# Order of stores and loads on one queue, y's parts in two portions, a fifth product read through a copy, and a denser first pair

## The chip, the cores and the metric

The kernel runs on one core of one Trainium2 chip. TensorE (PE) multiplies matrices into PSUM banks, VectorE (DVE), ScalarE (ACT) and GpSimd (POOL) work on tiles, and SyncE (SP) issues most of the DMAs. The metric is the device time of one execution in microseconds; lower is better.

## The reference

Three stages follow one another on 3072 tokens of 512 features. The stage that the change is about is the last, here called MoE2.

```python
for t in range(S):                                   # per head, decayed linear attention
    state = gamma * state + k_t (outer) v_t
    y[t] = scale * q_t @ state
h = x @ w_in;  x = (h - tanh(h)) @ w_out             # MoE1, d_ff = 2048
h = x @ w_in2                                        # MoE2, d_ff = 1024
e = exp(h - max(h));  sm = e / (sum(e) + 1e-9)
solu = h * sm
ln = (solu - mean(solu)) / sqrt(var(solu) + 1e-6) * g_ln
out = ln @ w_out2
```

## The kernel before

All products are made as three matmuls of a high and a low part each (hi x hi, hi x lo, lo x hi). MoE2 works on 12 pairs of 128-token tiles; pair j has the odd tile 2j+1 and the even tile 2j.

*First product of MoE2.* `Pair.part` makes the 7 products P1, P2, P6, P5, P7, P4, P3 of a Strassen scheme; each is `product2` (L922), 6 matmuls of 128x512 into a PSUM bank. Bank q1 gathers P1, P6 and P7 on top of one another, bank q3 gathers P5 and P3. After P1, P6 and P7 `keep2` (L929) has ScalarE copy q1 as it then is to a tile `part`. `add_half` (L937) has VectorE add a bank and a `part` to one half of a tile hn of h, with its minimum (nm). After P7 VectorE makes the odd tile's second half from q3 (then P5 alone) and P7's copy, so P3, which goes on in q3, has to wait for that reading.

*The middle.* `soft` makes exp (ScalarE, L947), the product with h (VectorE, L949), hn (ScalarE, L951), the squares (ScalarE, L953) and a block transpose (VectorE, L955), stores the tile to memory as `ud` (SyncE, L956), and GpSimd ends with the row scale `sc`. `turn` (L969) loads it back as hn<-ud in the transposed order, 128x32x32. `trans` splits it into uh (a ScalarE cast, L160) and ul (VectorE, L161).

*Second product.* `outp` is 24 matmuls into po (L986), three for each of 8 slices: uh, uh, ul. ScalarE scales the result to ob (L990) and issues the DMA to out.

*Inputs of a pair.* `load_y` (SyncE, L468) loads yl, `sum_y` has GpSimd make ysum from it (four instructions, L482 to L485), and `split_y` splits both: ScalarE casts yha (2 instructions) and yhs (one, 128x1024, L498), GpSimd subtracts for yla (3) and yls (4, L475). ya serves P1, P2 and P4, ys serves P5, P6, P7 and P3.

*Order.* Pair 0 lies between the last steps f of MoE1's second product (`products_y`, 12 matmuls a step, L377); ysb are ScalarE's and VectorE's copies of its PSUM banks. Pairs 1 to 11 come behind it: TensorE's order is that of the code (`manual_schedule`): pair j, then the two output tiles of pair j-1, up to pair 9; then pair 10, pair 11 and all the outputs left. On the other engines a scheduler sets the order; `pin` keeps an instruction where the code has it among others pinned on its engine.

Of the kernel before, what the change touches and what calls it, by code (L numbers as in the profile page):

```python
# [26 lines left out]
F32 = mybir.dt.float32  # L27
# [9 lines left out]
P = 128  # L37
# [51 lines left out]
def body(ctx: ExitStack, tc, z, w_in, w_out, w_in2, w_out2, g_ln, cst, tab, out):  # L89
# [14 lines left out]
    def t4(shape, dtype, name):  # L104
        return big.tile(shape, dtype, tag="t4", name=name)
# [365 lines left out]
    def on_pool(n, out, a, b, op):  # L471
        k = out.shape[1] // n
        for i in range(n):
            at = slice(i * k, (i + 1) * k)
            nc.gpsimd.tensor_tensor(out[:, at], a[:, at], b[:, at], op)  # L475

    def sum_y(j):
        t = yl[j]
        a11, a12, a21, a22 = (t[:, i, k : k + 2, :] for i in range(2) for k in (0, 2))
        s = ysum[j] = t4([P, 4, 2, P], F32, "ysum")  # L480
        s1, s2, s3, s4 = (s[:, i, :, :] for i in range(4))
        nc.gpsimd.tensor_tensor(s1, a21, a22, ALU.add)  # L482
        nc.gpsimd.tensor_tensor(s2, s1, a11, ALU.subtract)
        nc.gpsimd.tensor_tensor(s3, a11, a21, ALU.subtract)
        nc.gpsimd.tensor_tensor(s4, a12, s2, ALU.subtract)  # L485

    def split_y(j):
        t, s = yl.pop(j), ysum.pop(j)
        a22 = t[:, 1, 2:4, :]
        ya, ys_ = ([t4([P, 4, 2, P], F32R, f"y{n}{g}") for n in "hl"] for g in "as")  # L490
        flat = "p a k t -> p (a k t)"
        for to, lo, n, src in (
            (ya, 0, 2, t[:, 0, :, :].rearrange("p k t -> p (k t)")),
            (ya, 2, 1, a22.rearrange("p k t -> p (k t)")),
            (ys_, 0, 4, s.rearrange(flat)),
        ):
            h, o = (w[:, lo : lo + n, :, :].rearrange(flat) for w in to)
            nc.scalar.copy(h, src)  # L498
            on_pool(n, o, src, h.bitcast(F32), ALU.subtract)
        at = {P1: (ya, 0), P2: (ya, 1), P4: (ya, 2)}  # L500
        at |= {P5: (ys_, 0), P6: (ys_, 1), P7: (ys_, 2), P3: (ys_, 3)}
        ys[j] = {m: [w[:, i, :, :] for w in to] for m, (to, i) in at.items()}


    wl, xs, sums = {}, {}, {}
# [410 lines left out]
    def product2(j, m, ph, first=True):  # L916
        a = ys[j][m]
        n = 0
        for r in range(2):
            bh, bl = com.w[m, r]  # L920
            for x, w in ((a[0], bh), (a[0], bl), (a[1], bh)):
                nc.tensor.matmul(  # L922
                    ph, x[:, r, :], w, start=first and n == 0, stop=n == 5, skip_group_check=True
                )
                n += 1
# [9 lines left out]
    def add_half(h, half, ph, part, seen):  # L935
        hn, nm = h
        nc.vector.tensor_tensor_reduce(  # L937
            hn[:, half * 512 : (half + 1) * 512], ph, part, -1.0,
            3.0e38 if seen is None else nm[seen], ALU.add, ALU.min, nm[half],
        )  # L940

    def soft(i, h, last):

        hn, nmx = h[0], h[1][last]
        ex = t4([P, FF2], F32, "ex")
        ssum = sp.tile([P, 1], F32, tag="ssum", name="ssum")
        nc.scalar.activation(ex, hn, AF.Exp, bias=nmx, scale=-1.0, accum_out=ssum)  # L947
        us = sp.tile([P, 1], F32, tag="us", name="us")
        nc.vector.scalar_tensor_tensor(ex, hn, 1.0, ex, ALU.mult, ALU.mult, accum_out=us)  # L949
        nc.vector.tensor_scalar(us, us, -1.0 / FF2, None, ALU.mult)  # L950
        nc.scalar.activation(hn, ex, AF.Identity, bias=us)  # L951
        ssq = sp.tile([P, 1], F32, tag="ssq", name="ssq")
        nc.scalar.activation(ex, ex, AF.Square, bias=us, accum_out=ssq)  # L953

        nc.vector.transpose(ex, hn)  # L955
        nc.sync.dma_start(out=ud[i], in_=ex)  # L956

        nc.vector.tensor_scalar(ssum, ssum, 1e-9, -1.0, ALU.add, ALU.mult)
        nc.vector.reciprocal(ssum, ssum)
        nc.vector.tensor_scalar(ssq, ssq, ssum, ssum, ALU.mult, ALU.mult)  # L960
        nc.vector.tensor_scalar(ssq, ssq, 1.0 / FF2, 1e-6, ALU.mult, ALU.add)
        sc = sp.tile([P, 1], F32, tag="sc", name="sc")
        nc.gpsimd.tensor_tensor(sc, ssq, mhalf, ALU.pow)
        nc.gpsimd.tensor_tensor(sc, sc, ssum, ALU.mult)
        uc[i], sc2[i] = hn, sc

    def turn(j):
        for i in (2 * j + 1, 2 * j):
            nc.sync.dma_start(  # L969
                out=uc[i].rearrange("p (c i b) -> p c i b", c=NF2, i=B),  # L970
                in_=ud[i].rearrange("(i a) (g c b) -> (a g) c i b", i=B, g=4, c=NF2),
            )

    def trans(i):
        u = uc.pop(i)
        uh, ul = (t4([P, NF2 * P], F32R, "u" + n) for n in "hl")
        parts(uh, ul, u, nc.vector)
        ut[i] = [w.rearrange("p (f t) -> p f t", f=NF2) for w in (uh, ul)]
# [15 lines left out]
    class Pair:  # L994
# [5 lines left out]
        def part(self, m):  # L1000
            j = self.j
            if m == P1:
                self.q1 = bank2()
                product2(j, P1, self.q1)
                self.kept = keep2(self.q1)
            elif m == P2:
                q = bank2()
                product2(j, P2, q)
                add_half(self.b, 0, q, self.kept, None)
            elif m == P6:  # L1010
                product2(j, P6, self.q1, False)
                self.u2 = keep2(self.q1)
            elif m == P5:
                self.q3 = bank2()
                product2(j, P5, self.q3)
            elif m == P7:
                product2(j, P7, self.q1, False)
                self.kept = keep2(self.q1)
                add_half(self.a, 1, self.q3, self.kept, None)
            elif m == P4:  # L1020
                q = bank2()
                product2(j, P4, q)
                add_half(self.a, 0, q, self.kept, 1)
                soft(2 * j + 1, self.a, 0)
            else:
                product2(j, P3, self.q3, False)
                add_half(self.b, 1, self.q3, self.u2, 0)
                soft(2 * j, self.b, 1)
                ys.pop(j)
# [5 lines left out]
    for n, (s, f) in enumerate(steps):  # L1035
        if n:
            if f == 0:
                y_banks(s)
                if s == NSB - 1:
                    bank_of[:] = [(ps_a, "r"), (ps_a, "r"), (ps_h, "h"), (ps_h, "h")]  # L1040
            load_g(n + 5)
            load_wo(n + 4)
            if n + 2 < len(steps):
                split_p(n + 2)
            if n + 2 < NF1:
                split_wo(n + 2)
            products_y(f, gp.pop(n), wo[f], py)
        if f == NF1 - 1:
            keep_y(s, py)
        if s >= NSB - 3 and n % 2 == 0 and com.n[2] < 12:  # L1050
            com.step()
        m = n - 2 * NF1 - 6
        if m >= 0 and m % 3 == 0:
            step2(m // 3)
        if s == NSB - 1:
            if f == 0:
                load_y(0)
            if f == 2:
                sum_y(0)
                load_y(1)  # L1060
            if f == 5:
                split_y(0)
            if f == 9:
                sum_y(1)
                load_y(2)
            if f == 8:
                pair = Pair(0)
            for m in {8: (P1, P2), 9: (P6,), 10: (P5,), 11: (P7,), 12: (P4,), 13: (P3,)}.get(f, ()):
                pair.part(m)
            if f == 12:  # L1070
                split_y(1)
            if f == 13:
                turn(0)
            if f == 14:
                sum_y(2)
    G.close()
    M.close()


    ps_2 = ctx.enter_context(tc.tile_pool(name="ps_2", bufs=6, space=PSUM, reuse_waits="tile"))  # L1080
    ps_o = ctx.enter_context(tc.tile_pool(name="ps_o", bufs=2, space=PSUM, reuse_waits="tile"))
    NJ = NTT // 2
    bank_of[:] = [(ps_2, "h2")]
    load_y(3)
# [1 line left out]
    def pair_of(j, before):  # L1086
        pair = Pair(j)
        for n, m in enumerate((P1, P2, P6, P5, P7, P4, P3)):
            if n == 0 and j + 1 < NJ:
                split_y(j + 1)  # L1090
            if n == 2 and j + 2 < NJ:
                sum_y(j + 2)
            if n == 4 and j + 3 < NJ:
                load_y(j + 3)
            if n == 5 and before is not None:
                trans(2 * before + 1)
            pair.part(m)
        turn(j)
        if before is not None:
            trans(2 * before)  # L1100
# [75 lines left out]
```

## Time and profile before

| | us |
|---|---|
| median of 3 runs | 865.69 |
| the 3 runs | 864.72 to 869.44 |
| profiled execution | 867.15 |
| its span | 865.4 |
| TensorE busy in the span | 829.4 (96%) |
| VectorE, ScalarE, GpSimd busy | 540.7, 461.2, 291.6 |

The span is the time from the first to the last recorded instruction. An engine's row in a timeline gives its start, its duration and, in brackets, how long the engine had been idle before it and what ended that. A row with x2 stands for two instructions that follow one another.

### The profile page before, as it was taken

What the parts mean: (1) busy time and instruction counts of PE and PEld (TensorE: products, weight loads), DVE (VectorE), ACT (ScalarE), POOL (GpSimd) and SP (SyncE); (2) the same over time, 40 slices, a digit from 0 to 9 for tenths busy, and PEclk for the clock granted to TensorE, in tenths of its full rate; (3) what the DMA queues carried; (4) which work ended last, traced back from release to release, by engine and by line L of the source; (5) the groups of instructions that cost most, each with busy time, mean ns of one, the idle gap of its engine ahead of it and who ended that gap; (6) DMA issues with size and microseconds to landing.
All of it is one profiled execution on the core that took longest, in us unless ns stands there. A gap on an engine that the chain in (4) does not pass through costs nothing.

```text
span 865.4 us, 16366 instructions
## 1 busy us (share of the span) xinstructions
PE 829.4 (96%) x6296; PEld 675.4 (78%) x6296; DVE 540.7 (62%) x999; ACT 461.2 (53%) x868; POOL 291.6 (34%) x304
## 2 busy tenths in 40 slices
PE   5799999999999899999999999999899999999898
PEld 4678888788877687888788888888577777777786
DVE  3788975999858757223573979473555455555561
ACT  4655744646555546444462627244566666666662
POOL 4411100180634348433300350142544444444210
PEclk9899999999999899999999999999899999999999
DMA  9658654344899626955584647440766666665574
GB/s 361 254 215 301 254 190 156 120 147 177 303 362 335 236 82 223 411 198 174 195 337 127 226 121 281 148 169 25 171 145 147 147 147 145 146 147 122 121 162 105
DMA packets 168460, 169.41 MB, mean 196 GB/s; under 512 B 105664, under 2 KB 117952, under 8 KB 168384
## 3 DMA queue, kind: packets, MB, share of 16 engines
q1 hardware_dynamic: 160032, 153.38, 57.1%
q10 hardware_dynamic: 8352, 15.00, 4.7%
q8 instruction: 49, 0.80, 0.4%
q14 instruction: 27, 0.22, 0.1%
HBM read 107.02 MB, written 61.34 MB: 195 GB/s over the span
## 4 chain that ended last, share of the span: by engine, by line
PE 81%; DVE 5%; DMA 4%; ACT 3%; issue 3%; POOL 2%; SPq 0%; ACTq 0%; POOLq 0%; DVEq 0%
PE py L377 29%; PE ph L750 15%; PE po L986 14%; PE ph L922 11%; PE ph L352 8%; PE out L228 2%; DMA hn<-ud 2%; PE sc L228 2%; DMA z<-z 1%; DMA raw<-w_in 1%; ACT part L929 1%; POOL hs L768 1%; DVE hn L937 1%; POOL yls L475 1%; ACT uh L160 0%
## 5 line engine op out<-in xcount | busy, mean ns | idle before, releaser
L377 PE MATMUL py<-gp,w 128*128 128x512 f32 x768 | 175.4, 389 | 0.0
L377 PEld LDWEIGHTS py<-gp,w 128*128 128x128 f32 x768 | 144.1, 188 | 29.9
L986 PE MATMUL po<-w,uh 128*128 128x512 f32 x384 | 118.6, 390 | 0.0
L768 POOL TENSOR_TENSOR hs<-hs,th 128x512 f32<-128x512 f32 x48 | 66.8, 1395 | 95.8 <-ACT th L766 91.1
L986 PEld LDWEIGHTS po<-w,uh 128*128 128x128 f32 x384 | 72.1, 188 | 14.8
L352 PE MATMUL ph<-xh,w 128*128 128x512 f32 x256 | 82.1, 395 | 0.8 <-DVE w L154 0.8
L377 PE MATMUL py<-gh,w 128*128 128x512 f32 x256 | 79.2, 390 | 0.3 <-ACT gh L365 0.3
L986 PE MATMUL po<-w,ul 128*128 128x512 f32 x192 | 76.4, 398 | 0.6 <-DVE us L950 0.6
L153 ACT CAST w<-wf 128x512 fp32r<-128x512 f32 x70 | 43.1, 621 | 57.6 <-DVE wf L144 47.1
L922 PE MATMUL ph<-w,yhs 128*128 128x512 f32 x192 | 63.9, 416 | 6.4 <-ACT part L929 5.8
L475 POOL TENSOR_TENSOR yla<-yl,yha 128x256 fp32r<-128x256 f32 x36 | 26.3, 756 | 127.2 <-ACT yha L498 127.2
L766 ACT ACTIVATE th<-hs 128x512 f32<-128x512 f32 x48 | 30.3, 631 | 60.4 <-DVE hs L776 52.4
L937 DVE CUSTOM_DVE_ANT_0 hn<-ph,part 128x512 f32<-128x512 f32 x24 | 16.6, 691 | 72.5 <-ACT part L929 54.9
L154 DVE TENSOR_TENSOR w<-wf,w 128x512 fp32r<-128x512 f32 x70 | 51.2, 736 | 15.3 <-ACT w L153 14.5
L161 DVE TENSOR_TENSOR gp<-g,gp 128x512 fp32r<-128x512 f32 x64 | 48.4, 770 | 18.8 <-ACT gp L160 18.6
L750 PE MATMUL ph<-xh,wch 128*128 128x512 f32 x140 | 57.3, 409 | 1.6 <-DVE hs L776 1.6
L352 PEld LDWEIGHTS ph<-xh,w 128*128 128x128 f32 x256 | 48.0, 188 | 11.8 <-DVE w L154 1.3
L377 PEld LDWEIGHTS py<-gh,w 128*128 128x128 f32 x256 | 48.0, 188 | 10.6 <-ACT gh L365 0.7
L929 ACT COPY part<-ph 128x512 f32<-128x512 f32 x36 | 21.1, 586 | 64.7 <-PE ph L922 64.7
L750 PE MATMUL ph<-xh,wcl 128*128 128x512 f32 x140 | 55.4, 396 | 0.0
L750 PE MATMUL ph<-xl,wch 128*128 128x512 f32 x140 | 55.3, 395 | 0.0
L776 DVE TENSOR_TENSOR hs<-ph,part 128x512 f32<-128x512 f32 x48 | 32.9, 686 | 35.2 <-PE ph L750 20.8
(123 smaller groups left out, 1811.9 us busy)
## 6 DMA issues: line engine op xcount, KB each, us to landing
z<-z SPq DMA_DIRECT2D x48, 512.0 KB, 6.4
g<-gd SPq DMA_DIRECT2D x64, 256.0 KB, 5.3
raw<-w_in SPq DMA_DIRECT2D x24, 512.0 KB, 6.3
raw<-w_out SPq DMA_DIRECT2D x24, 512.0 KB, 4.4
gd<-hs SPq DMA_DIRECT2D x48, 256.0 KB, 3.9
ud<-ex SPq DMA_DIRECT2D x24, 512.0 KB, 4.5
hn<-ud SPq DMA_DIRECT2D x24, 512.0 KB, 5.8
y1d<-ysb SPq DMA_DIRECT2D x24, 256.0 KB, 3.9
```

The source lines that it names most:

```text
L153: pin(nc.scalar.copy(hi, wf), fixed)
L154: pin(eng.tensor_tensor(lo, wf, hi.bitcast(F32), ALU.subtract), fixed)
L161: eng.tensor_tensor(o, src, h.bitcast(F32), ALU.subtract)
L228: pin(nc.tensor.matmul(o, a, b, start=True, stop=True, skip_group_check=True), held[0])
L352: nc.tensor.matmul(ph, a[:, k, :], x, start=n == 0, stop=n == 3 * NK - 1), s < 2
L377: nc.tensor.matmul(py[e], a[:, cols], x, start=f == 0 and n == 0, stop=f == NF1 - 1 and n == 2)
L475: nc.gpsimd.tensor_tensor(out[:, at], a[:, at], b[:, at], op)
L750: nc.tensor.matmul(ph, a, x, start=first and n == 0, stop=n == 5, skip_group_check=True)
L768: eng.tensor_tensor(g, h, th, ALU.subtract)
L776: nc.vector.tensor_tensor(h, ph, part, ALU.add)
L922: nc.tensor.matmul(ph, x[:, r, :], w, start=first and n == 0, stop=n == 5, skip_group_check=True)
L986: nc.tensor.matmul(po, a[:, f, :], b, start=f == 0 and n == 0, stop=f == NF2 - 1 and n == 2)
```

## The change

Four things are changed. `pin` is put around the stores `ud` and the loads of hn, so that SyncE issues both stores of a pair, then both loads, then yl. `split_y` gets an argument for its two portions: portion 0 (yha, yla) is asked for after P1 of the pair before, portion 1 (yhs, yls) after P6, and `sum_y` after P7. P5's result is copied by ScalarE (`p5`), and the odd tile's second half is made from q1 and that copy. The first pair takes four steps of products_y (P1 P2, P6 P5, P7 P4, P3) where it took six, with its other calls moved to match, and the two PSUM pools of the last stage are opened in the other order.

```diff
-    def split_y(j):
-        t, s = yl.pop(j), ysum.pop(j)
...
+    def split_y(j, halves=(0, 1)):
         flat = "p a k t -> p (a k t)"
...
+        for g in halves:
+            y = [t4([P, 4, 2, P], F32R, f"y{n}{'as'[g]}") for n in "hl"]
+            if g:
+                todo = ((0, 4, ysum.pop(j).rearrange(flat)),)
+                at = {P5: 0, P6: 1, P7: 2, P3: 3}
+            else:
+                t = yl[j]
+                todo = (
+                    (0, 2, t[:, 0, :, :].rearrange("p k t -> p (k t)")),
+                    (2, 1, t[:, 1, 2:4, :].rearrange("p k t -> p (k t)")),
+                )
+                at = {P1: 0, P2: 1, P4: 2}
+            for lo, n, src in todo:
+                h, o = (w[:, lo : lo + n, :, :].rearrange(flat) for w in y)
+                nc.scalar.copy(h, src)
+                on_pool(n, o, src, h.bitcast(F32), ALU.subtract)
+            ys.setdefault(j, {}).update({m: [w[:, i, :, :] for w in y] for m, i in at.items()})
...
-        nc.sync.dma_start(out=ud[i], in_=ex)
+        pin(nc.sync.dma_start(out=ud[i], in_=ex))
...
-            nc.sync.dma_start(
+            pin(nc.sync.dma_start(
                 out=uc[i].rearrange("p (c i b) -> p c i b", c=NF2, i=B),
                 in_=ud[i].rearrange("(i a) (g c b) -> (a g) c i b", i=B, g=4, c=NF2),
-            )
+            ))
...
                 product2(j, P5, self.q3)
+                self.p5 = keep2(self.q3)
             elif m == P7:
                 product2(j, P7, self.q1, False)
                 self.kept = keep2(self.q1)
-                add_half(self.a, 1, self.q3, self.kept, None)
+                add_half(self.a, 1, self.q1, self.p5, None)
...
-            if f == 5:
+            if f == 4:
                 split_y(0)
+            if f == 6:
+                sum_y(1)
             if f == 9:
-                sum_y(1)
                 load_y(2)
...
-            for m in {8: (P1, P2), 9: (P6,), 10: (P5,), 11: (P7,), 12: (P4,), 13: (P3,)}.get(f, ()):
+            for m in {8: (P1, P2), 9: (P6, P5), 10: (P7, P4), 11: (P3,)}.get(f, ()):
                 pair.part(m)
+            if f == 9:
+                split_y(1)
+            if f == 11:
+                sum_y(2)
             if f == 12:
-                split_y(1)
-            if f == 13:
                 turn(0)
-            if f == 14:
-                sum_y(2)
...
+    ps_o = ctx.enter_context(tc.tile_pool(name="ps_o", bufs=2, space=PSUM, reuse_waits="tile"))
     ps_2 = ctx.enter_context(tc.tile_pool(name="ps_2", bufs=6, space=PSUM, reuse_waits="tile"))
-    ps_o = ctx.enter_context(tc.tile_pool(name="ps_o", bufs=2, space=PSUM, reuse_waits="tile"))
...
-            if n == 0 and j + 1 < NJ:
-                split_y(j + 1)
-            if n == 2 and j + 2 < NJ:
+            if n == 5 and before is not None:
+                trans(2 * before + 1)
+            pair.part(m)
+            if n in (0, 2) and j + 1 < NJ:
+                split_y(j + 1, (n // 2,))
+            if n == 4 and j + 2 < NJ:
                 sum_y(j + 2)
             if n == 4 and j + 3 < NJ:
                 load_y(j + 3)
-            if n == 5 and before is not None:
-                trans(2 * before + 1)
-            pair.part(m)
         turn(j)
```

The first place is ScalarE's order where products_y ends and pair 1 begins. ph_6969 is bank q1 of pair 1 in the kernel before, so its three copies are those of P1, P6 and P7; yhs is that of pair 2.

```order
L498 CAST yha<-yl 128x256
L387 COPY ysb<-py 128x512 x2
L951 ACTIVATE hn<-ex,us 128x1024
L953 ACTIVATE ex,ssq<-ex,us 128x1024
L498 CAST yhs<-ysum 128x1024
L929 COPY part<-ph_6969 128x512 x3
L160 CAST uh<-hn 128x1024
```

In the changed kernel ph_6957 is q1 and ph_6996 is q3.

```order
L954 ACTIVATE hn<-ex,us 128x1024
L956 ACTIVATE ex,ssq<-ex,us 128x1024
L387 COPY ysb<-py 128x512 x2
L932 COPY part<-ph_6957 128x512
L503 CAST yhs<-ysum 128x1024
L932 COPY part<-ph_6957 128x512
L932 COPY part<-ph_6996 128x512
L932 COPY part<-ph_6957 128x512
L160 CAST uh<-hn 128x1024
```

The copy of P1's result moves from behind the yhs cast to ahead of it, pair 0's last hn and Square move ahead of the ysb copies, and the copy of P5 is new.

The second place is SyncE's order in a steady pair (pair 5, tiles 11 and 10). ud11 and ud10 are the stored tiles, hn what is loaded from them.

```order
L956 DMA ud11_148<-ex_7769 128x1024
L969 DMA hn_7689<-ud11_148 128x32x32
L956 DMA ud10_147<-ex_7794 128x1024
L468 DMA yl_7931<-y1d4_135 128x1024
L969 DMA hn_7692<-ud10_147 128x32x32
```

In the changed kernel:

```order
L959 DMA ud11_148<-ex_7781 128x1024
L959 DMA ud10_147<-ex_7806 128x1024
L972 DMA hn_7699<-ud11_148 128x32x32
L972 DMA hn_7702<-ud10_147 128x32x32
L468 DMA yl_7954<-y1d4_135 128x1024
```

The second store moves ahead of the first load, and the second load ahead of yl.

At the same place of a steady pair (pair 2) VectorE makes the halves of hn. In the kernel before ph2_7184 is q3, part_7199 is P7's copy, and ph2_7206 holds P4; the bracket names the engines that a row waits for.

```order
L937 ISA hn_7134,nm_7136<-ph2_7184,part_7199 128x512 [waits Activation_49]
L937 ISA nm_7136 128x1
L937 ISA hn_7134,nm_7135<-ph2_7206,part_7199,nm_7136 128x512 [waits DVE_49,PE_49]
L937 ISA nm_7135 128x1
L161 TENSOR_TENSOR ul_7203<-hn_6949,uh_7202 128x1024 [waits DMAHW3_49,Activation_49]
```

In the changed kernel ph2_7144 is q1, part_7190 the copy of P5 and part_7198 that of P7.

```order
L940 ISA hn_7138,nm_7140<-ph2_7144,part_7190 128x512 [waits Activation_49]
L940 ISA nm_7140 128x1
L940 ISA hn_7138,nm_7139<-ph2_7212,part_7198,nm_7140 128x512 [waits DVE_49,PE_49]
L940 ISA nm_7139 128x1
L161 TENSOR_TENSOR ul_7209<-hn_6951,uh_7208 128x1024 [waits DMAHW4_49,Activation_49]
```

The first half reads q1 in place of q3; its place and the engine that it waits for stay.

The third place is ScalarE's order from the end of pair 10 to pair 11, the last. ph_8740 is q1 of pair 11.

```order
L160 CAST uh<-hn 128x1024
L947 ACTIVATE ex,ssum<-hn,nm 128x1024 x2
L160 CAST uh<-hn 128x1024
L929 COPY part<-ph_8740 128x512
L951 ACTIVATE hn<-ex,us 128x1024
L953 ACTIVATE ex,ssq<-ex,us 128x1024
L951 ACTIVATE hn<-ex,us 128x1024
L929 COPY part<-ph_8740 128x512
```

In the changed kernel ph_8762 is q1 of pair 11 and ph_8787 its q3.

```order
L160 CAST uh<-hn 128x1024
L950 ACTIVATE ex,ssum<-hn,nm 128x1024
L932 COPY part<-ph_8762 128x512
L950 ACTIVATE ex,ssum<-hn,nm 128x1024
L160 CAST uh<-hn 128x1024
L954 ACTIVATE hn<-ex,us 128x1024
L932 COPY part<-ph_8762 128x512
L956 ACTIVATE ex,ssq<-ex,us 128x1024
L932 COPY part<-ph_8787 128x512
```

The copy of P1's result moves from behind the second uh cast to ahead of the second exp, and that of P6 ahead of both Squares.

## Rows read from the trace of the kernel before

**Rows 1.** Stages: start:end length, busy of PE, PEld, DVE, ACT, POOL, PE clock, DMA share, GB/s.
```profile
606.40:624.30 17.90, 13.84 (x46) 10.27 (x46) 7.81 (x18) 7.75 (x11) 12.24 (x20) 0.81 0.96 206
624.30:812.60 188.30, 187.24 (x802) 148.46 (x800) 97.31 (x230) 120.75 (x178) 80.18 (x131) 1.00 0.63 143
812.60:828.60 16.00, 13.54 (x50) 10.29 (x50) 11.79 (x31) 10.64 (x16) 0.74 (x2) 0.89 0.45 81
```

**Rows 2.** Chain of waits: start, duration, what ran; the last outputs.
```profile
828.56 32.65 PE po L986 x144
```

**Rows 3.** Timeline of the hand-over: start, duration, instruction, idle time before it.
```profile
605.82 1.05 ACT L387 COPY ysb<-py 128x512 f32<-128x512 f32 x2
...
606.93 0.73 PE L922 MATMUL ph<-w,yha 128*128 128x512 f32 x2 [0.52 <-ACT ysb L387]
...
608.25 1.15 ACT L953 ACTIVATE ex<-ex,us 128x1024 f32<-128x1024 f32 x1
...
611.77 1.04 ACT L498 CAST yhs<-ysum 128x1024 fp32r<-128x1024 f32 x1 [2.28 <-POOL ysum L485]
...
612.72 0.58 ACT L929 COPY part<-ph 128x512 f32<-128x512 f32 x1
...
613.35 1.22 PE L922 MATMUL ph<-w,yhs 128*128 128x512 f32 x2 [3.41 <-ACT part L929]
...
623.99 0.50 PE L986 MATMUL po<-w,ul 128*128 128x512 f32 x1
```

**Rows 4.** Groups of instructions, TensorE, 613.4 to 619.3: count, busy, mean ns, idle before.
```profile
L922 PE MATMUL ph<-w,yhs 128*128 128x512 f32 x10 | 5.2, 624 | 3.4 <-ACT part L929 3.4
```

**Rows 5.** Timeline of a steady pair, around its P4 and P3.
```profile
641.56 0.59 ACT L929 COPY part<-ph 128x512 f32<-128x512 f32 x1 [2.13 <-PE ph L922]
...
642.04 1.05 ACT L160 CAST uh<-hn 128x1024 fp32r<-128x1024 f32 x1
642.18 0.69 DVE L937 CUSTOM_DVE_ANT_0 hn<-ph,part 128x512 f32<-128x512 f32 x1 [3.89 <-ACT part L929]
...
642.50 0.39 PE L922 MATMUL ph<-w,yla 128*128 128x512 f32 x1
...
642.94 0.73 PE L922 MATMUL ph<-w,yhs 128*128 128x512 f32 x2
...
643.70 1.22 DVE L161 TENSOR_TENSOR ul<-hn,uh 128x1024 fp32r<-128x1024 f32 x1
...
644.98 0.50 PE L986 MATMUL po<-w,ul 128*128 128x512 f32 x1
...
663.91 0.73 PE L922 MATMUL ph<-w,yhs 128*128 128x512 f32 x2
```

**Rows 6.** Groups of instructions, 624.3 to 812.6: the uh casts.
```profile
L160 ACT CAST uh<-hn 128x1024 fp32r<-128x1024 f32 x18 | 18.9, 1050 | 8.8 <-DMA hn<-ud 8.8
```

**Rows 7.** Timeline of SyncE in a steady pair: start of the issue, its duration.
```profile
673.45 0.32 SPq L956 DMA_DIRECT2D ud<-ex  x1
676.13 0.58 SPq L969 DMA_DIRECT2D hn<-ud  x1
677.14 2.69 SPq L956 DMA_DIRECT2D ud<-ex  x1
...
684.50 0.59 SPq L969 DMA_DIRECT2D hn<-ud  x1
```

**Rows 8.** Timeline of TensorE around the last pair.
```profile
812.77 0.73 PE L922 MATMUL ph<-w,yhs 128*128 128x512 f32 x2
...
819.50 0.72 PE L922 MATMUL ph<-w,yhs 128*128 128x512 f32 x2 [2.35 <-ACT part L929]
...
828.40 0.62 PE L986 MATMUL po<-w,uh 128*128 128x512 f32 x2
```

**Rows 9.** The page's DMA issues: count, KB each, median us from issue to landing.
```profile
ud<-ex SPq DMA_DIRECT2D x24, 512.0 KB, 4.5
hn<-ud SPq DMA_DIRECT2D x24, 512.0 KB, 5.8
```

More of the change, by code (lines that the diff above doesn't have):

```diff
@@ L485, in sum_y @@
         nc.gpsimd.tensor_tensor(s4, a12, s2, ALU.subtract)
-    def split_y(j):
-        t, s = yl.pop(j), ysum.pop(j)
-        a22 = t[:, 1, 2:4, :]
-        ya, ys_ = ([t4([P, 4, 2, P], F32R, f"y{n}{g}") for n in "hl"] for g in "as")
+    def split_y(j, halves=(0, 1)):
         flat = "p a k t -> p (a k t)"
[L492 to L502, printed above, removed]
+        for g in halves:
[15 more added lines that the diff above has]
+            ys.setdefault(j, {}).update({m: [w[:, i, :, :] for w in y] for m, i in at.items()})
     wl, xs, sums = {}, {}, {}
```

## The prediction, made before the changed kernel ran

> **What bounds the kernel now.** I read the stage table first. TensorE is busy for 187.24 of 188.30 us in the long steady stretch from 624.3 to 812.6, but for only 13.84 of 17.90 us around the hand-over to the last stage (606.4 to 624.3) and 13.54 of 16.00 us around the last pair (812.6 to 828.6); in both short stretches its granted clock is below one as well, 0.81 and 0.89 [rows 1]. So TensorE sets the time, and a change can gain only where TensorE stands still or runs slowly. The price of a matmul with nothing in its way comes from the end of the chain of waits, where 144 of them take 32.65 us: 0.2267 us each [rows 2]. Whatever starts further apart than that is lost, and I looked up what ended each of these waits in the timelines.
>
> *Hand-over.* Pair 1's P6 waits 3.41 us, with ScalarE's copy of P1's result as releaser [rows 3]. That copy takes 0.58 us and P1 had long ended: it starts at 612.72, as soon as the yhs cast ahead of it is through, and that cast had waited 2.28 us for GpSimd's ysum. The matmuls after that wait run at half speed: ten of them show 624 ns [rows 4], where one elsewhere shows 0.39 us [rows 5]. The clock fell after TensorE had stood still.
>
> *Steady pairs.* From one P3 to the next, 642.94 to 663.91, a pair takes 20.97 us [rows 5]; its 90 matmuls (42 of the pair, 48 of two output tiles) cost 20.40. What is lost every time is around P3: it starts 0.44 after the last P4 matmul (642.50), because VectorE reads bank q3 from 642.18 on, having waited for ScalarE's copy of P7's result (641.56 plus 0.59); and the output's third matmul (644.98) waits for the ul that VectorE makes after the two halves of hn [rows 5]. Besides, ScalarE's 18 uh casts wait 8.8 us in all for the loads of hn [rows 6]. The cause is SyncE's queue: load odd goes out at 676.13, store even behind it takes 2.69 us to issue, and load even must wait for that store to land, so it leaves only at 684.50 [rows 7].
>
> *Last pair.* The same picture: in ScalarE's order P1's copy stands behind the cast of uh even, P6 waits 2.35 us for that copy [rows 8], and the stretch has its granted clock of 0.89.
>
> **The change part by part.** *First pair in four steps, and split_y in two portions: the hand-over.* In the kernel before, P3 of pair 0 stands behind five blocks of 12 products_y matmuls, now behind three, so pair 0's work on ScalarE, VectorE and GpSimd comes 2 x 12 x 0.2267 = 5.4 us earlier. Its second Square, at 608.25 for 1.15 [rows 3], would then end at 604.0. The two ysb copies, 1.05 us [rows 3] and now behind it in ScalarE's order, end by 605.1, and pair 1's P1 needs them at 606.93 - 0.52 = 606.4: 1.3 us to spare, so the 0.52 us wait ahead of P1 goes too. P1's copy now stands directly behind the ysb copies and ahead of the yhs cast, so it ends about 0.6 after P1, some 0.8 before P2 is through, and P6 finds it done. The yhs cast, 1.04 us, moves in between P1's and P6's copies, and the ysum that it reads is asked for at step 11 instead of 14, 3 x 12 x 0.2267 = 8.2 us earlier. Copy, cast and P6's copy need 2.2 us, and P6 ends 2.7 after P1, so it is hidden by P2 and P6. What would be late next is ul, as in every steady pair. Size: from 606.41 to the third output matmul at 623.99 [rows 3] are 17.58 us for 44 matmuls, worth 9.97. Of the 7.6 lost, about 0.5 stays (the ul wait with the matmul slowed behind it). Gain **7.1**.
>
> *P5 copied by ScalarE.* Adds 12 copies at 0.59 us [rows 5], 7.1 us of ScalarE, which has idle time in every pair: its P7 copy comes 2.13 us after it had nothing to do [rows 5], and the new copy fits there. What it takes away is P3's wait for VectorE's read of q3: 0.44 - 0.23 = 0.21, and 0.11 for a slower next matmul, 0.32 in a pair. But it is not kept. VectorE's first half now reads q1 and the copy of P5; ScalarE's copy of P7 reads q1 at that very time, and the order of VectorE still shows that half waiting for ScalarE. So the halves come when they did, ul too, and the output's third matmul waits 0.3 longer instead. I take 0 for pairs 1 to 9; the ends are 0 and 9 x 0.32 = 2.9. After pairs 10 and 11 no output matmul follows at once, so there the 0.32 counts (in the sum for the tail).
> The Trainium skill, "PSUM — Partial Sum Buffer", section "PSUM bank collisions raise a hardware error", says that no two engines may access one bank and quadrant at a time, two reads included, and that software has to order them. By that rule the two reads of q1 cannot overlap, which speaks against the gain of 2.9 and for 0.
>
> *Stores and loads on SyncE.* Before: store odd, load odd, store even, yl, load even. Now both stores, then both loads, then yl. In the pair shown [rows 7], store odd leaves at 673.45 and has landed by 676.13, 2.7 later. Store even is ready by about then and no longer stands behind load odd; with 2.7 to 4.5 to land [rows 7, 9], load even leaves at 679 to 681 rather than 684.50. The nine even casts among the 18 wait up to 1.0 us each [rows 6]; a load 3.5 us earlier ends that. Its worth on TensorE is the excess of the pairs: eight periods from 642.94 [rows 5] to 812.77 [rows 8] take 169.83, eight undisturbed ones 167.76. Gain **2.0**. The price is on load odd: it now leaves after store even, about 0.4 us later, and its pieces stand behind the store's 512 KB. A load takes 5.8 us [rows 9], so 676.1 + 0.4 + 5.8 = 682.3, and up to 2.7 more (the store's time) = 685.0. Its cast was at 642.04 [rows 5], which is 684.0 two periods on. I take 683.5, since a store alone lands within 2.7, of which its bytes are only a part: no wait, but only 0.5 to spare. If it does wait, uh may end 0.6 later without harm (cast to 643.09, ul from 643.70 [rows 5]). yl goes behind everything; it is first read in the next pair.
>
> *Last pair.* ScalarE now has P1's copy ahead of uh even and of the even exp, and the yhs cast is out of the way. From P3 of pair 10 (812.77) to the outputs (828.40) are 15.63 us for 48 matmuls, 10.88: lost 4.75, and with the two P3 waits (one of 0.21 ahead of 812.77) 4.96 [rows 8]. What stays: P6's copy now stands behind the even exp, uh even and hn. With 1.15 for exp and hn, as for Square [rows 3], and 1.05 for uh, it ends 0.59 + 1.15 + 1.05 + 1.15 + 0.59 = 4.5 after P1, and P2, P6 and P5 last 4.1: P7 waits 0.45, and 0.11 for a slowed matmul. And the first ul of the outputs stands behind a transpose on VectorE: between 0 and 1.2, one instruction of ul's size (643.70 [rows 5]); I take 0.9, as the halves of hn queue there too. Gain **3.5**.
>
> *Swapped PSUM pools.* No instruction is added, and pair 1's P1 still takes the bank that the first ysb copy frees: 0.
>
> Sum: 7.1 + 2.0 + 3.5 = 12.6. The profiled execution took 867.15 us, 1.5 above the median; 867.15 - 12.6 = 854.55, and from the median 865.69 - 12.6 = **853.1 us**.
>
> **The rivals.** *A, P3's gain is kept.* If VectorE starts its halves earlier than ScalarE's P7 copy allows now, 2.9 more: 850.2. For it: 0.3 us are plainly lost at each P3. Against: the order's wait on ScalarE.
>
> *B, the hand-over only half mended.* Pair 0's loads go out in a stretch in which the DMA engines are 96% busy [rows 1]. Moved 5.4 earlier, the second transpose's store leaves at about 605.4 and the first at 603.5; with 4.5 for a store and 5.8 for a load [rows 9] load odd lands at 613.8. ScalarE's cast is due 0.46 ahead of the last P4 matmul as at 642.04 [rows 5]: 606.4 + 35 x 0.2267 - 0.46 = 613.9. If it lands 3 us later, the first output waits some 2.5 us, and half speed may follow a wait of that length (it did after 2.35 and after 3.41), another 2.5 us: 855.6 to 858.1.
>
> *C, load odd late in every pair, the one that ends slower.* Load odd's 512 KB now follow store even's in the same queue. If it lands after 684.0, ScalarE waits, ul is late, and and behind the 0.6 us of slack each us costs one. The gain of 12.6 is used up at 12.6 / 10 pairs = 1.3 us each: load odd landing at 685.9, 0.9 beyond my upper bound. At 686.5, 1.9 a pair, it gives 853.1 + 19 = 872. At the upper bound, 685.0, it costs 0.4 a pair: 857.
> The Trainium skill, "DMA: Bandwidth & Descriptors", section "Queues, rings and completion order", says that each DMA engine consumes the descriptors of a queue in ring order. By that, load odd's data cannot start before store even's, and C's smaller form, 857, would come rather than 853; no run here shows yet by how much load odd is late.
>
> *D, no effect.* The copies ahead of P6 could be held by something else again, for example by ysb or by pair 0's exp on ScalarE, with the same 3 us wait; only the gain of SyncE's queue remains: 863.7.
>
> **How the numbers follow.** Forecast, 851.5 to 855.5: 0.50. A, near 850: 0.10. B, 855.6 to 858.1: 0.17. C small, near 857: 0.10; C slower, near 872: 0.04. D: 0.09. The range leaves out D and the slower C. It reaches from A's 850.2, less 0.7 should load even's gain be larger than the periods say, to B's 858.1, and 1.4 above for the ul wait in the tail at its upper end and a small C with B: **849.5 to 859.5**. A measurement of this kernel can tell about 0.5%, 4.3 us, from no change: faster means below 861.4, which takes in all but D and the slower C: 0.87; same 0.09; slower 0.04.
>
> **What would show it right or wrong.** In the stage table after, the hand-over should show a granted clock of one or nearly, and no wait of P6 for ScalarE above 0.3. P3 should start 0.23 after the last P4 matmul, and the third output matmul of each pair be late by about 0.6, not 0.3: if it is late by less, A is right. On SyncE load even should leave within 5 us of store even; uh casts of even tiles should not wait, and those of odd tiles neither: if they wait, C. If pair periods come out at 20.97, the steady part is right; shorter means A, longer C. A granted clock below one anywhere behind 606 would show B or D. The forecast is wrong if the first output of pair 0 waits for a load, or if ScalarE's copies queue behind something that I moved.

## The result: 852.6 us, the forecast was 853.1

| | median us | runs | ratio to before, 95% interval |
|---|---|---|---|
| before | 866.23 | 864.72 to 869.44 | |
| changed kernel | 852.58 | 851.57 to 857.47 | 0.985, 0.980 to 0.990 |

The profiled execution took 853.42 us, its span is 851.5. TensorE is busy for 820.1 us of it, as against 829.4; matmuls at half speed account for a part of the difference, and 3.0 us of it lie in the steady pairs, where the clock is granted in full in both. The stage table of the changed kernel, cut near the points of [rows 1] (columns as there; here pair 1's P1 starts at 605.55, pair 10's P3 at 802.59 and the last outputs at 813.97):

```profile
606.40:616.60 10.20, 9.92 (x44) 7.90 (x44) 4.03 (x11) 5.48 (x8) 5.65 (x8) 1.00 1.27 226
616.60:800.00 183.40, 181.17 (x790) 147.34 (x789) 95.91 (x227) 123.86 (x184) 80.23 (x131) 1.00 0.71 150
800.00:816.00 16.00, 15.80 (x70) 12.75 (x69) 12.39 (x30) 13.27 (x21) 1.17 (x3) 1.00 0.40 65
```

The clock is granted in full in all three, where [rows 1] had 0.81 and 0.89. What TensorE still waits for from 570 us on (engine and line, what it waited for: us in all, times, longest):

```profile
PE po L989 <- DVE ul L161: 2.5, 9, 0.3
PE po L989 <- DVE ssq L964: 0.4, 1, 0.4
PE ph L925 <- ACT part L932: 0.2, 1, 0.2
```

The waits of 3.41 and 2.35 us for ScalarE's copy [rows 3, 8] have become 0.2, and the longest row is now ul, nine times. The hand-over in the timeline, TensorE and ScalarE:

```profile
605.55 0.61 PE L925 MATMUL ph<-w,yha 128*128 128x512 f32 x2
...
607.11 0.59 ACT L932 COPY part<-ph 128x512 f32<-128x512 f32 x1 [1.45 <-PE ph L925]
...
607.60 1.05 ACT L503 CAST yhs<-ysum 128x1024 fp32r<-128x1024 f32 x1
...
608.27 0.61 PE L925 MATMUL ph<-w,yhs 128*128 128x512 f32 x2
...
613.04 1.05 ACT L160 CAST uh<-hn 128x1024 fp32r<-128x1024 f32 x1
```

P1 (605.55) has no wait, its copy starts when P1 ends, ahead of yhs, and P6 (608.27) starts 12 matmuls after P1 without a gap. The first uh cast shows no wait for its load either. A steady pair, to be held against [rows 5]:

```profile
676.41 0.39 PE L925 MATMUL ph<-w,yla 128*128 128x512 f32 x1
676.63 0.61 PE L925 MATMUL ph<-w,yhs 128*128 128x512 f32 x2
...
676.93 0.75 DVE L940 CUSTOM_DVE_ANT_0 hn<-ph,part,nm 128x512 f32<-128x512 f32 x1
...
677.61 1.22 DVE L161 TENSOR_TENSOR ul<-hn,uh 128x1024 fp32r<-128x1024 f32 x1
...
677.99 0.61 PE L989 MATMUL po<-w,uh 128*128 128x512 f32 x2
...
678.89 0.50 PE L989 MATMUL po<-w,ul 128*128 128x512 f32 x1 [0.28 <-DVE ul L161]
```

The first output matmul of the pair of [rows 5], in the kernel before:

```profile
644.43 0.62 PE L986 MATMUL po<-w,uh 128*128 128x512 f32 x2
```

P3 starts 0.22 after the last P4 matmul, not 0.44. But ul starts 1.20 after that matmul, as before (643.70 - 642.50), and the third output matmul, 0.90 after the first and not 0.55 (644.98 - 644.43), gives the gain back.

**Stages.** I cut every run at three starts of TensorE: pair 0's P1, the first output matmul of pair 0 and that of pair 8; the last column ends with the span. In the changed kernel these are 576.99, 615.07, 782.98 and 851.48, in the kernel before 577.69, 623.45, 793.20 and 865.36; the same instructions of the other traces give the rest. "Steady" is eight pair periods.

| kernel | median us | hand-over | steady | last pairs | sum |
|---|---|---|---|---|---|
| before | 866.23 | 45.76 | 169.75 | 72.16 | 287.67 |
| changed | 852.58 | 38.08 | 167.91 | 68.50 | 274.49 |
| changed, again (e10) | 854.50 | 38.08 | 167.86 | 68.49 | 274.43 |
| without P5's copy (e1) | 856.54 | 38.42 | 167.86 | 70.23 | 276.51 |
| P5's copy in the last two pairs only (e9) | 855.94 | 38.43 | 167.90 | 68.31 | 274.64 |
| without the pins (e2) | 861.62 | 38.08 | 171.76 | 71.82 | 281.66 |
| before, with the pins alone (e12) | 867.46 | 44.67 | 171.85 | 70.92 | 287.44 |
| split_y whole (e3) | 859.71 | 40.62 | 173.69 | 69.18 | 283.49 |
| pair 0 in six steps (e4) | 861.43 | 42.90 | 169.82 | 68.74 | 281.46 |
| pools in the old order (e8) | 855.19 | 38.41 | 167.98 | 68.57 | 274.96 |
| half ahead of P7's copy (e5) | 859.06 | 38.07 | 170.84 | 70.18 | 279.09 |
| ul last (e6) | 851.73 | 38.08 | 164.67 | 67.18 | 269.93 |
| ul one slice later (e11) | 850.48 | 38.08 | 164.81 | 67.63 | 270.52 |

### The profile page after: what moved, and what is told of

Read it like the earlier page. It is cut to its first block, busy times and chain, and to the rows that moved or that the text cites. A ratio compares the mean times of both kernels' runs of the same rounds, so it can differ in the third digit from the quotient of the medians.

```text
span 851.5 us, 16381 instructions
## 1 busy us (share of the span) xinstructions
PE 820.1 (96%) x6296; PEld 672.9 (79%) x6296; DVE 536.0 (63%) x999; ACT 468.2 (55%) x880; POOL 291.2 (34%) x304
## 4 chain that ended last, share of the span: by engine, by line
PE 84%; DVE 5%; DMA 4%; issue 3%; ACT 2%; POOL 1%; SPq 0%; ACTq 0%; DVEq 0%; POOLq 0%
PE py L377 30%; PE ph L753 16%; PE po L989 14%; PE ph L352 10%; PE ph L925 10%; PE out L228 3%; PE sc L228 2%; DVE ul L161 1%; DMA z<-z 1%; DVE hn L940 1%; DMA raw<-w_in 1%; DMA wcd<-wch 1%; ACT part L932 1%; DMA hn<-ud 1%; POOL hs L771 0%
## 5 line engine op out<-in xcount | busy, mean ns | idle before, releaser
L925 PE MATMUL ph<-w,yhs 128*128 128x512 f32 x192 | 59.2, 390 | 0.2 <-ACT part L932 0.2
L160 ACT CAST gp<-g 128x512 fp32r<-128x512 f32 x64 | 38.6, 618 | 30.8 <-DMA g<-gd 18.4
```

What stands on the lines that cost most here:

```text
L925: nc.tensor.matmul(ph, x[:, r, :], w, start=first and n == 0, stop=n == 5, skip_group_check=True)
```

## Experiments

The kernel before took 866.74 us beside e1 to e4, 867.15 beside e5, e6, e8 and e9, 869.62 beside e10 and e11, 867.45 beside e12.

**The same kernel again (e10).** 

> The changed kernel once more, unaltered, as the measure for the run beside it and for what the stretch ahead of pair 0 does from run to run: in the runs so far pair 0's P1 started between 576.2 and 580.8 us, while from there to the end a kernel's stages repeated within a few tenths. Theory: from pair 0's P1 to the end 274.5 us again, the whole time 852.6 to 855. Rival (the difference lies in the kernels, not in the runs): P1 at 577.0 and 852.6 again.

854.50 us (853.19 to 856.37), ratio 0.984 (0.981 to 0.986). In its profiled execution pair 0's P1 starts here:

```profile
579.96 0.62 PE L925 MATMUL ph<-w,yha 128*128 128x512 f32 x2
```

That is 3.0 us later than in the first one, and from there to the end the two agree within 0.06. So whole times of this kernel carry 2 to 3 us that come from the part ahead of pair 0, and below I argue from the stages.

**P5's copy undone (e1).**

```diff
-                self.p5 = keep2(self.q3)
...
-                add_half(self.a, 1, self.q1, self.p5, None)
+                add_half(self.a, 1, self.q3, self.kept, None)
```

> The changed kernel without the copy of P5: VectorE's first half reads q3 and P7's copy again. Theory (the copy is worth nothing in pairs 1 to 9): P3 starts 0.44 us after the last P4 matmul again instead of 0.23, and the output's third matmul comes 0.32 after the one before instead of 0.67, so the pair period stays 20.97; only pairs 10 and 11 lose 0.3 each. 853.2 us against 852.6. Rival (P3's wait was worth its full price): 0.32 in each of 11 pairs, 856.1.

The median alone, 856.5, is the rival's number; the stages say otherwise. The steady part is 167.86 against 167.91: not a tenth a pair. The loss is in the last pairs (1.7) and at the hand-over (0.3: the boundary lies between P3's wait of pair 1 and the next ul's). ScalarE and TensorE there, e1:

```profile
807.88 1.03 ACT L160 CAST uh<-hn 128x1024 fp32r<-128x1024 f32 x1
808.81 0.57 ACT L932 COPY part<-ph 128x512 f32<-128x512 f32 x1
...
809.44 0.74 PE L925 MATMUL ph<-w,yhs 128*128 128x512 f32 x2 [1.09 <-ACT part L932]
...
813.28 0.73 PE L925 MATMUL ph<-w,yhs 128*128 128x512 f32 x2 [0.79 <-ACT part L932]
```

and ScalarE of the changed kernel at the same place:

```profile
805.51 0.59 ACT L932 COPY part<-ph 128x512 f32<-128x512 f32 x1 [0.58 <-PE ph L925]
806.00 1.16 ACT L950 ACTIVATE ex<-hn,nm 128x1024 f32<-128x1024 f32 x1
807.14 1.04 ACT L160 CAST uh<-hn 128x1024 fp32r<-128x1024 f32 x1
```

Without P5's copy the scheduler puts P1's copy of pair 11 behind exp and uh again, so P6 waits 1.09 us and P7 0.79 (0.20 in the changed kernel). P3 of pairs 10 and 11 is late again too, by 0.8 us with the slowed matmuls, but the late matmul ahead of the last outputs, 0.7 in the changed kernel, is gone. So the copy's net worth comes mostly from a place in ScalarE's order in one pair.

**P5's copy in the last two pairs only (e9).**

```diff
-                self.p5 = keep2(self.q3)
+                self.p5 = keep2(self.q3) if j >= NTT // 2 - 2 else None
...
+                add_half(self.a, 1, *((self.q1, self.p5) if self.p5 is not None else (self.q3, self.kept)), None)
```

> The changed kernel with P5's copy in pairs 10 and 11 only; pairs 0 to 9 read q3 and P7's copy as in the kernel before. Theory (the copy is worth nothing in a steady pair, and its whole worth is in ScalarE's order around pair 11, where P1's copy stands ahead of the even exp): pairs 1 to 9 take 20.97 us with 0.44 ahead of P3 and 0.32 ahead of the third output matmul, the last pair is as in the changed kernel: 852.6 us, the same. Rival (the copy is worth 0.3 in each pair): 855.5.

Stages 38.43, 167.90, 68.31: nothing is lost without the other ten copies, in the steady part or at the end. The theory holds by stages. The median of 855.9 is nearer to the rival's 855.5, but in the profiled execution pair 0's P1 starts at 580.84, 3.9 us later than in the changed kernel's, and that difference lies ahead of everything that was altered.

**The half ahead of P7's copy (e5).**

```diff
-                self.kept = keep2(self.q1)
                 add_half(self.a, 1, self.q1, self.p5, None)
+                self.kept = keep2(self.q1)
```

> The changed kernel with the odd tile's second half asked for ahead of ScalarE's copy of P7, not behind it: VectorE reads q1 first, ScalarE after it, and in VectorE's order ul now comes between the two halves. Theory (in the changed kernel that half starts late only because both engines read bank q1, and the output's third matmul waits for it through ul): the half starts about 0.6 us earlier, ul with it, the gap of 0.67 in front of the output's third matmul goes to 0.23 in pairs 1 to 9, pairs take 20.4 us: 847.5 us against 852.6. Rival (the half waits for something else, or the later exp of the odd tile is late next): gap 0.67 as before, or pairs still 20.97 with another wait in them, 852 to 857.

In pair 1 (P1 at 608.75), and behind it the same half in the changed kernel (P1 at 605.55):

```profile
615.86 0.69 DVE L940 CUSTOM_DVE_ANT_0 hn<-ph,part 128x512 f32<-128x512 f32 x1 [3.38 <-PE ph L925]
616.60 0.58 ACT L932 COPY part<-ph 128x512 f32<-128x512 f32 x1
616.73 1.23 DVE L161 TENSOR_TENSOR ul<-hn,uh 128x1024 fp32r<-128x1024 f32 x1 [0.17 <-ACT uh L160]
617.87 0.74 DVE L940 CUSTOM_DVE_ANT_0 hn<-ph,part,nm 128x512 f32<-128x512 f32 x1
...
618.72 1.15 ACT L950 ACTIVATE ex<-hn,nm 128x1024 f32<-128x1024 f32 x1 [1.54 <-DVE nm L940]
```

```profile
613.17 0.69 DVE L940 CUSTOM_DVE_ANT_0 hn<-ph,part 128x512 f32<-128x512 f32 x1 [3.89 <-ACT part L932]
```

VectorE's half is now released by TensorE and starts 7.11 after P1 instead of 7.62, though it reads the same two things. So its wait for ScalarE was the order of two readings of q1, not a want of data. The mechanism is shown, but the rival was right that no time is gained, and more is lost than it said (859.06 us; 4.6 by stages): the other half moves behind ul, exp starts 9.97 after P1 (9.32 in the changed kernel), stores and loads follow, and ScalarE's uh casts wait for loads again (groups of instructions from 624 to 812, e5 and then the changed kernel):

```profile
L160 ACT CAST uh<-hn 128x1024 fp32r<-128x1024 f32 x17 | 17.8, 1047 | 17.4 <-DMA hn<-ud 17.4
```

```profile
L160 ACT CAST uh<-hn 128x1024 fp32r<-128x1024 f32 x18 | 18.8, 1044 | 0.0
```

**The pins undone (e2), and alone (e12).**

```diff
-        pin(nc.sync.dma_start(out=ud[i], in_=ex))
+        nc.sync.dma_start(out=ud[i], in_=ex)
```

(and the same for the loads of hn; e12 is the kernel before with these pins added.)

> The changed kernel without the pins: SyncE's order is store odd, load odd, store even, load even again (yl stays behind them). Theory (the order of the queue is worth the 2 us of the steady part): store even takes over 2 us to issue again, load even leaves 3 us later, ScalarE's uh cast of the even tile waits for it by 0.5 to 1.3 us, pairs take 21.0 to 21.3, and P7 of pair 11 waits about 1 us longer, since P6's copy stands behind that cast: 854.5 to 856. Rival (taking yhs out of ScalarE's middle already brought the stores forward enough): no wait of uh, 852.6.

> The kernel before with the pins alone: SyncE issues store odd, store even, load odd, yl, load even. Theory (the queue's order pays only together with yhs's move out of ScalarE's middle): store even is ready 1 us later than in the changed kernel and yl now goes between the loads, so load odd is late by some tenths and load even gains little; the hand-over stays as it was. From pair 0's P1 to the end 286.5 to 289 us against 287.7. Rival (the term of the prediction holds by itself: even casts no longer wait, odd ones neither): 285.7 or less, the steady pairs 20.97.

Undone, they cost 7.2 us by stages, twice the most that I had expected: 3.9 in the steady pairs and 3.3 at the end, where the last outputs too wait for a late load. SyncE in e2:

```profile
669.32 0.32 SPq L959 DMA_DIRECT2D ud<-ex  x1
672.01 0.59 SPq L972 DMA_DIRECT2D hn<-ud  x1
672.69 3.33 SPq L959 DMA_DIRECT2D ud<-ex  x1
680.87 0.59 SPq L972 DMA_DIRECT2D hn<-ud  x1
```

Store even takes 3.33 us to issue behind load odd, and load even leaves 8.2 us after that store's issue began. In the changed kernel (a row with x2 gives the time from the first start to the second end):

```profile
665.12 3.06 SPq L959 DMA_DIRECT2D ud<-ex  x2
668.28 4.72 SPq L972 DMA_DIRECT2D hn<-ud  x2
```

both stores are out by 668.2 and both loads by 673.0. Alone, the pins are worth nothing: 867.46 us beside 867.45, ratio 1.000 (0.998 to 1.003), and the steady pairs are 2.1 us slower. The 1.1 us less at its hand-over are no merit of the pins: P6 waits 3.42 us there, as against 3.41, but only about 8 matmuls behind it run at half speed, not 12. In this kernel yhs is still in ScalarE's middle, and yl goes out between the loads (SyncE, e12):

```profile
674.28 4.02 SPq L956 DMA_DIRECT2D ud<-ex  x2
678.47 0.58 SPq L969 DMA_DIRECT2D hn<-ud  x1
679.16 4.83 SPq L468 DMA_DIRECT2D yl<-y1d  x1
684.09 0.59 SPq L969 DMA_DIRECT2D hn<-ud  x1
```

Load odd leaves 4.19 us after store odd instead of 3.16, load even 9.81 after it (11.05 in [rows 7]), and the uh casts of both tiles wait:

```profile
L160 ACT CAST uh<-hn 128x1024 fp32r<-128x1024 f32 x17 | 17.8, 1048 | 13.5 <-DMA hn<-ud 13.5
```

This is rival C, in its small form.

**split_y as one (e3).** The last loop is that of the kernel before again:

```diff
+            if n == 0 and j + 1 < NJ:
+                split_y(j + 1)
+            if n == 2 and j + 2 < NJ:
+                sum_y(j + 2)
+            if n == 4 and j + 3 < NJ:
+                load_y(j + 3)
...
             pair.part(m)
-            if n in (0, 2) and j + 1 < NJ:
-                split_y(j + 1, (n // 2,))
-            if n == 4 and j + 2 < NJ:
-                sum_y(j + 2)
-            if n == 4 and j + 3 < NJ:
-                load_y(j + 3)
```

> The changed kernel with split_y asked for as one again, ahead of P1, and sum_y after P2: the yhs cast is back in ScalarE's middle, ahead of the even tile's hn, and yl goes out between the two loads. Theory (at the hand-over the earlier ysum counts, not the place of the cast): P6 of pair 1 does not wait, clock 1.00 there; in the steady pairs store even comes 0.85 later and load even some 3 us later, which costs 0 to 0.3 a pair: 852.6 to 855.5. Rival (the place of the cast behind P1's copy is what mended the hand-over): P6 of pair 1 waits 2 us or more and half speed follows, 856 to 858.

P6 of pair 1 does not wait, as the theory said; but neither account saw what came next:

```profile
608.28 0.33 SPq L959 DMA_DIRECT2D ud<-ex  x1
608.71 0.66 SPq L972 DMA_DIRECT2D hn<-ud  x1
...
617.38 1.04 ACT L160 CAST uh<-hn 128x1024 fp32r<-128x1024 f32 x1 [3.38 <-DMA hn<-ud]
...
618.48 0.73 PE L989 MATMUL po<-w,uh 128*128 128x512 f32 x2 [2.38 <-ACT uh L160]
```

With yhs, 1.04 us, ahead of pair 0's last hn, its even store misses its place ahead of three y1d stores on SyncE, and the first load leaves at 608.71, 2.3 after pair 1's P1 (606.42), where the changed kernel has it 0.1 after (605.63 against 605.55). The output waits 2.38 us, and half speed follows. In the steady pairs loads are late as in e12 (yl goes between them here too). Behind pair 0's P1 9.0 us are lost.

**Pair 0 in six steps (e4).** The table of steps and the calls around it are those of the kernel before.

> The changed kernel with pair 0 in six steps of products_y again and its splits, sums and turn at their old steps; the two portions, the pins, P5's copy and the pools stay. Theory (the hand-over's gain is the 5.4 us by which pair 0 is done earlier): ysum and the loads of pair 0 come 5 us later again; ScalarE's first uh cast waits some 4 us for its load, P7 of pair 1 about 1 us for P6's copy, and half speed may follow: 857 to 860. Rival (the yhs cast behind P1's copy is enough): P6 doesn't wait and the first output is late by 1 us at most, 852.6 to 853.6.

As the theory said: 7.0 us, 4.8 of it ahead of the first output and 1.9 behind it. P6 and P7 wait 0.54 and 0.35, then ScalarE waits 3.83 us for a load and TensorE 2.83 for that cast; the next matmuls are at half speed:

```profile
619.48 1.04 ACT L160 CAST uh<-hn 128x1024 fp32r<-128x1024 f32 x1 [3.83 <-DMA hn<-ud]
620.58 0.73 PE L989 MATMUL po<-w,uh 128*128 128x512 f32 x2 [2.83 <-ACT uh L160]
```

**The pools in the old order (e8).** 

> The changed kernel with the two PSUM pools opened in the old order, so that P1 of pair 1 takes another bank of products_y. Theory: the bank is free in time either way, P1 of pair 1 does not wait, 852.6 us. Rival (P1 waits for VectorE's copy of its bank): 0.3 to 0.7 us ahead of P1, 853.2.

0.5 us by stages. Pair 1's P1 starts 0.16 late and the next matmul 0.11, together nearly the rival's 0.3; small, and not told apart in the whole time.

**The wait that is left: ul last (e6), and one slice later (e11).** e6 makes an output tile's 16 matmuls with uh first; e11 puts each slice's ul matmul behind the next slice's uh matmuls:

```diff
-        for f in range(NF2):
...
-            for n, (a, b) in enumerate(((uh, bh), (uh, bl), (ul, bh))):
+        for f in range(NF2 + 1):
+            for n in range(3):
+                at = f if n < 2 else f - 1
```

> The changed kernel with the 24 matmuls of an output tile in another order: the 16 with uh first, the 8 with ul last, so that ul is wanted 3.6 us after the first output matmul instead of 0.45. Theory (all that is left between 20.40 and 20.97 in a pair is this wait for ul): no gap above 0.3 in pairs 1 to 9, pairs 20.4 us, and most of the 0.7 at the last outputs goes too: 847 us. Rival (uh, the loads or ScalarE become the bound as soon as pairs are shorter): pairs 20.6 to 20.9, 849 to 852.

> The changed kernel with each output slice's ul matmul behind the next slice's two uh matmuls, so that the first ul is wanted as the fifth matmul of a tile and not as the third; ScalarE's order, with both hn ahead of ob, stays as in the changed kernel, unlike with all ul last. Theory (ul is 0.44 us late in a steady pair, and two matmuls are worth 0.45): no gap above 0.3 in pairs 1 to 9, pairs 20.4 us, from pair 0's P1 to the end 274.5 - 9 x 0.57 - 0.6 = 268.8 us; 5.7 us faster than the unaltered one beside it. Rival (shorter pairs leave the odd tile's load too late, as with all ul last): pairs 20.5 to 20.7, 3 to 4.5 us faster.

By stages both beat both kernels. In whole time this is clear for e11: 850.48 us beside 854.50 for the unaltered kernel in the same runs, ratio to before 0.979 (0.977 to 0.981) against 0.984 (0.981 to 0.986); e6's 0.983 (0.980 to 0.986) can't be told from the changed kernel's. By stages e11 saves 3.9 us of the 5.7 expected: steady periods are 20.60 us, not 20.40, as its rival said. uh waits for some loads again (e11, then e6):

```profile
L160 ACT CAST uh<-hn 128x1024 fp32r<-128x1024 f32 x18 | 18.8, 1046 | 1.7 <-DMA hn<-ud 1.6
```

```profile
L160 ACT CAST uh<-hn 128x1024 fp32r<-128x1024 f32 x18 | 18.9, 1048 | 5.6 <-DMA hn<-ud 5.3
```

In e6, where the loads are waited for most, they are the next limit, as the rival said: of the 1.4 us by which its eight periods exceed undisturbed matmuls, 1.3 lie at the odd tile's first two. In e11 only 0.2 of 1.6 lie there, and 1.2 at the odd tile's first ul matmul and the one behind it, so ul is still just late:

```profile
661.62 0.49 PE L990 MATMUL po<-w,ul 128*128 128x512 f32 x1
661.95 0.62 PE L990 MATMUL po<-w,uh 128*128 128x512 f32 x2
```

The second starts 0.33 after the first, not 0.23. What of this comes from the loads, through uh, stays open. Which of the two kernels is faster was not settled.

## Why the prediction was right

**Sum.** Forecast 12.6; by the medians 13.65, by the profiled spans 13.9. Of these 0.7 lie ahead of pair 0's P1 (577.69 before), within what e10 shows there; 13.2 lie behind it.

**Hand-over, 7.1.** Measured 7.7, of which 0.3 is P3's wait of pair 1, given back at the next ul: 7.4. The steps held: ysb in time, P1's copy ahead of yhs, full clock. e4 and e3 show both halves of the reason. Without the denser steps the loss of 7 us returns, at the load instead of at P6; without the portions ysum is in time, but the load is not. Rival B was nearer than its 0.17 said: 1 us more on ScalarE in pair 0 was enough to bring it about (e3).

**P5's copy, 0 in steady pairs.** Right (e1, e9), and for the stated reason (e5). The Trainium skill, "PSUM — Partial Sum Buffer", section "PSUM bank collisions raise a hardware error", has it that software must keep two engines' accesses to one bank apart; here the trace agrees as far as it goes: in e5 the half ends at 615.86 + 0.69 = 616.55 and ScalarE's copy starts at 616.60, so the two readings don't overlap there either (ScalarE was busy with uh until then, too). Rival A is out. What was mis-sized is the copy's share at the end: I put 0.64 there, as P3's waits of pairs 10 and 11, and it was 1.7, most of it through ScalarE's order.

**The queue, 2.0.** The number came out (169.75 - 167.91 = 1.84), and the wait that was to go is the one that went. By the starts of TensorE's matmuls, the eight periods before lose 2.6 us at P3, and 1.6 at the odd tile's and 1.7 at the even tile's first ul matmul and the one behind it; in the changed kernel 4.4 are lost at the odd tile's and nothing at P3 or the even tile's. (The nine even casts before waited between 0 and 1.85 us, not up to 1.0.) But the step behind the number did not hold, so that the match is in part luck: I had the order of stores and loads earn it by itself. Alone it earns nothing and costs 2.1 in the steady pairs (e12); with yhs out of ScalarE's middle and yl behind the loads it is worth 7.2 in all (e2). The failing piece is "store even is ready by about then": that is the doing of the portions, and I had priced them at the hand-over alone. Load odd was forecast with 0.5 us to spare; in the changed kernel no cast of the steady pairs waited (pair 0's second waited 0.67 and the last four 0.6 to 2.8, none with a wait of TensorE behind it), and what a page's row calls the median landing grew from 5.8 to 6.9 us [rows 9]:

```profile
ud<-ex SPq DMA_DIRECT2D x24, 512.0 KB, 3.1
hn<-ud SPq DMA_DIRECT2D x24, 512.0 KB, 6.9
```

Stores land sooner, 3.1 against 4.5, so the load behind them may take longer.

**Last pair, 3.5.** Measured 3.7 by stages. P7 comes 0.47 late (0.56 worked out), and the first ul of pair 10's tiles costs 0.7 instead of 0.9; that is the row for ssq above.

**The pools, 0.** P1 is a little late without the swap (e8): 0.3 us that I had not seen.

**Together.** Undone one by one, the parts are worth 2.0 (e1), 7.2 (e2), 9.0 (e3) and 7.0 (e4): 25 us, for a change that is worth 13.2, so the parts overlap. Three of them keep the same thing in time, the load of hn ahead of ScalarE's cast: without the pins or the portions it is late pair by pair, without the denser steps once, at the hand-over. e1 is the exception, where P1's copy in the last pair is late.

## What to carry to other kernels

Removing a wait on the bounding engine is worth only as much as the next thing in line allows: look for what releases the work behind it, here ul three matmuls later. Price a change of a queue's order by when its entries are ready, not only by their order; the same pins were worth nothing in the kernel before and 7 us in the changed one, where a cast on another engine and the load of yl stand elsewhere; which of the two matters more no run tells. When a kernel's total varies by more than the effect, cut each trace at the same instructions and compare the pieces.

## What the runs showed of the hardware

- Two executions of the same program reached the same instruction 3.0 us apart (576.99 and 579.96 us into the span), and from there ran 274.49 and 274.43 us.
- A 512 KB store behind a load of hn (128x32x32) in one queue took 2.69 us (before) and 3.33 us (e2) to issue in the pairs shown, instead of 0.32, and SyncE's next instruction started only after that.
- Half speed followed TensorE's waits of 2.35, 2.38, 2.83 and 3.41 us, with matmuls behind them at about twice their distance for 3 to 6 us; waits of 1.09 us (e1) and 1.14 us (e2) had none behind them.
